# Splitting the first weight load, gating loads behind DMA transposes, and masks of a second batch on TensorE, in a fused attention and feed-forward kernel

## The chip, the cores and the metric

The kernel runs on one core of one Trainium2 chip. The metric is the time of one execution in microseconds (us) on the device; a kernel is run several times and the median is quoted with its range. Most runs of one kernel agree within about 0.5% of their median. A few runs fall into a slower state and are left out of every ratio. Runs of two kernels that were measured together are called runs of the same rounds. The span in a profile is about 2 us shorter than the time.

In this kernel TensorE does the matmuls; VectorE and ScalarE do the elementwise work and the copies; GpSimd issues most loads; SyncE issues the stores of the output and the DMA transposes. A DMA is a transfer that runs beside the engines; it "lands" when its data can be used. PSUM is the memory that matmuls write to.

## The reference, cut to what matters

Eight batches of eight heads, 576 positions, head size 64. Half of the heads use a local causal mask of 32 positions, the other half a strided one. The attention output, 4608 tokens by 512, goes through a two-layer feed-forward with a squared ReLU.

```python
scores = scale * q @ k^T                      # per batch and head
mask_local   = (rel >= 0) & (rel < 32)        # heads 0..3
mask_strided = (rel >= 0) & (pos_k % 32 == pos_q % 32)   # heads 4..7
attn = softmax(where(mask, scores, -1e9))
x = (attn @ v) as [4608, 512]
h = x @ w_in                                  # 512 x 2048
g = s * relu(h)**2 + b
out = g @ w_out                               # 2048 x 512
```

## The kernel before

The kernel computes only the blocks of scores that the masks leave. It is laid out by a small planner in Python that runs when the kernel is built. The planner keeps an estimated clock `plan.t` for TensorE, an estimated time for every result, and picks for each small task the engine that should end it first. It fixes the order of the instructions on each engine; on the chip each engine takes its instructions in that order and waits where an input is not there yet. Attention matmuls of later batches are placed between feed-forward matmuls at a pace set by `batch_ns`.

The planner's choice of an engine and place (cut):

```python
def flush(self):
    ...                                   # the task whose inputs are planned to be ready first
    eng = min(p[1], key=lambda e: max(self.free[e], r) + p[1][e])
    end = max(self.free[eng], r) + p[1][eng]
    self.free[eng] = end
    p[2](eng)                             # emits the instruction now, in that engine's order
```

The loads of a batch. GpSimd issues all of them; `landing` is the planner's guess of when they arrive. For the local heads q and k are first rearranged (`qp`, `kp`) by ScalarE or VectorE:

```python
def fetch_qk(b):
    load_qk(b)                                        # nc.gpsimd.dma_start for ql, kl, qs, ks
    for name in ("q", "k"):
        plan.done["raw", name, b] = landing(1700)
        for mm in range(2):
            pair_post(b, name, mm, ("raw", name, b))  # the copies qp <- ql and kp <- kl
    for name in ("qs", "ks"):
        arrive(both(name, b), landing(2000))
...
# fetch_qk(b + 2) is posted once attention b has all its transposes:
last_t.after = when_all("t", b, lambda b=b: plan.post(
    [("fetch_v", b + 1) if b else ("free",)] +
    [("k", (b, mk)) for mk in range(4)], {"P": 0.0},
    lambda eng: fetch_qk(b + 2), [("fetch", b + 2)]))
```

From batch 2 on, k of the strided heads is transposed by a DMA that SyncE issues; before that by TensorE:

```python
by_dma = b >= 2
def k_dma(eng):
    st["k"] = qkp.tile([128, ST, SR], FP16, tag="kTs", name="kTs")
    nc.sync.dma_start_transpose(out=st["k"], in_=ks[b % 2][:, 1024 * mm:1024 * mm + 1024])
```

Masks: in batch 0 TensorE adds a large negative number to the scores by one more matmul; later VectorE multiplies the exponentials by a mask of 0 and 1:

```python
if b == 0:
    nc.tensor.matmul(out=..., lhsT=ident[0:nk, 0:nk],
                     rhs=neg_loc if loc else neg_str, start=True, stop=False)
nc.tensor.matmul(out=..., lhsT=..., rhs=..., start=b > 0, stop=True)
```

The weights w_in come in three transfers (512, 512 and 1024 columns), and attention is paced by the work of batch 1:

```python
for c, (at, n) in enumerate(((0, 512), (512, 512), (1024, 1024))):
    nc.gpsimd.dma_start(out=w_in_sb[c], in_=wv[:, :, at:at + n])
...
batch_ns = sum(s.ns for p in att[4:8] for s in p)
```

The softmax here doesn't subtract the row's maximum and nothing guards it: scores larger than these inputs give would overflow.

Of the kernel before, what the change touches and what calls it, by code (L numbers as in the profile page):

```python
# [9 lines left out]
FP16 = mybir.dt.float16  # L10
# [100 lines left out]
def kernel(  # L111
# [11 lines left out]
    nc = tc.nc  # L123
# [4 lines left out]
    scale = 1.0 / float(np.sqrt(D))  # L128
    PS = 512
    NFT = DFF // 128  # L130
    NBLK = NTOK // PS
# [11 lines left out]
    for p in range(SQ):  # L143
        for c in range(SQ):
# [26 lines left out]

    w_in_sb = [const.tile([128, 4, n], FP16, name=f"w_in_sb{i}")
               for i, n in enumerate((512, 512, 1024))]
    w_out_sb = const.tile([128, NFT, DM], FP16)
# [91 lines left out]

    def load_w_in():
        wv = moe_w_in.rearrange("(c p) f -> p c f", p=128)
        for c, (at, n) in enumerate(((0, 512), (512, 512), (1024, 1024))):
            nc.gpsimd.dma_start(out=w_in_sb[c], in_=wv[:, :, at:at + n])  # L270

# [25 lines left out]
    def cast_v(b, loc, mm, key):  # L297
        nt, np_, dst = (LT, 128, v_loc) if loc else (ST, SQ, v_str)

        def g(eng):  # L300
# [8 lines left out]

    TB, SB, AB, F1B, F2B = 1, 2, 1, 2, 2  # L310
    ps = {tag: [psum.tile([128, PS], FP32, name=f"ps_{tag}{i}") for i in range(n)]
          for tag, n in (("t", TB), ("s", SB), ("a", AB), ("f1", F1B), ("f2", F2B))}
# [19 lines left out]
    def pair_steps(b, m):  # L332
# [54 lines left out]

        by_dma = b >= 2

        def k_dma(eng):  # L390
            st["k"] = qkp.tile([128, ST, SR], FP16, tag="kTs", name="kTs")
            nc.sync.dma_start_transpose(out=st["k"], in_=ks[b % 2][:, 1024 * mm:1024 * mm + 1024])

        if by_dma and not loc:

            plan.post([("in", "ks", b, mm), ("s", (b - 1, m), 2)], {"D": 1000.0}, k_dma,
                      [("k", id_)])
        for name in ("q", "k"):
            if by_dma and not loc and name == "k":
                continue  # L400
            gr = group_of("t", b, m, True)
            for j in range(nt):
                steps.append(trans(name, j, gr))
# [4 lines left out]
        def score(i, group):  # L408
# [3 lines left out]
            def f():  # L412
                if i % per_s == 0:
                    st["s", g] = bank(group)
                c = i % per_s * 2 * nq
                if b == 0:

                    nc.tensor.matmul(
                        out=st["s", g][0:nk, c:c + 2 * nq], lhsT=ident[0:nk, 0:nk],
                        rhs=neg_loc if loc else neg_str, start=True, stop=False)  # L420
                nc.tensor.matmul(  # L421
                    out=st["s", g][0:nk, c:c + 2 * nq], lhsT=(st["k"][:, i * nq:i * nq + nk] if loc else st["k"][:, i, 0:SQ]),
                    rhs=st["q"][:, i].rearrange("d e c -> d (e c)"), start=b > 0, stop=True)

            s = Step(f, (2 if b == 0 else 1) * (2 * nq / 2.4 + 8), needs=[("q", id_), ("k", id_)],
                     group=group if i % per_s == 0 else None)
            if i % per_s == n - 1:
# [11 lines left out]
                def ms(eng):  # L439
# [8 lines left out]
                            [("p", id_, g)])]  # L448
                if b == 0:
                    s.posts = [([key], {"A": 170 + 0.83 * 2 * n * nq}, ex, [("p", id_, g), group])]  # L450
# [95 lines left out]

        if by_dma and loc:
            plan.post([("x", id_, e, nt - 1) for e in range(2)], {"D": 1000.0}, x_dma,
                      [("xT", b, m)])
        else:  # L550
            gr = group_of("t", b, m)
            for j in range(nt):
                steps.append(xtrans(j, gr))
# [5 lines left out]
    def ff1(T, ft, ct, group, cts=(0, 1, 2, 3), early=False):  # L559
        tok0 = T * PS  # L560
        def f():
            if ft == 0 and ct == cts[0]:
                gts[T] = gp.tile([128, NFT, PS], FP16, tag="gT", name="gT")
            if ct == cts[0]:
                gts["h", T, ft] = bank(group)
            nc.tensor.matmul(  # L566
                out=gts["h", T, ft], lhsT=w_in_sb[min(ft // 4, 2)][:, ct, :].rearrange(
                    "p (c x l) -> p c l x", x=128, l=4)[:, max(ft // 4 - 2, 0), ft % 4],
# [3 lines left out]
                 for c in ((ct,) if early else range(4))]  # L572
        needs.append(("w_in", ft // 4))
        if ft == 0 and ct == cts[0] and T >= 2:
# [60 lines left out]
    def arrive(keys, at):  # L635
        for k in keys:
            plan.done[k] = at
# [12 lines left out]

    def fetch_qk(b):
        load_qk(b)
        for name in ("q", "k"):
# [45 lines left out]
    def weights_in(eng):  # L699

        nonlocal ring
        nc.gpsimd.tensor_copy(out=gate[0:64, 2:4].bitcast(FP32), in_=vl_stage[64:128, 0, 0, 0:1])
        load_w_in()
        ring = 17700.0
        for keys, cost in ([0], 2900), ([1], 2900), ([2, 3], 5000):
            arrive([("w_in", c) for c in keys], landing(cost))

    plan.done[("first",)] = 13700.0
    plan.post([("first",)], {"P": 3500.0}, weights_in, [("w",)])
    plan.done["raw", "v", True, 0] = 16200.0  # L710
# [29 lines left out]
    for b in range(B):  # L740
        for m in range(4):
            steps, last_av, last_t = pair_steps(b, m)
            att.append(steps)
            if b + 2 < B:

                last_t.after = when_all("t", b, lambda b=b: plan.post(
                    [("fetch_v", b + 1) if b else ("free",)] +
                    [("k", (b, mk)) for mk in range(4)], {"P": 0.0},
                    lambda eng: fetch_qk(b + 2), [("fetch", b + 2)]))
# [5 lines left out]
    for T in range(NBLK):  # L755
        if T == 0:

            gr = [Group(*x) for x in (("s", SB), ("s", SB), ("f1", F1B), ("f1", F1B))]
            cts = (2, 0, 1, 3)
            f1 += [ff1(T, ft, ct, gr[ft], cts, True) for ct in cts for ft in range(4)]  # L760
# [122 lines left out]
```

## Time and profile before

| | before |
|---|---|
| time, median of 3 (range) | 330.31 us (329.79 to 330.5) |
| span of the profiled run (a fourth run, 330.79 us) | 328.9 us |
| TensorE busy | 97% |
| VectorE, ScalarE, GpSimd busy | 61%, 51%, 25% |
| first feed-forward matmul | 22.19 us |

In a timeline the columns are start, duration, engine, line, operation with output and input, and in brackets the idle time before it with what ended it.

```profile
70.94 0.68 POOL L240 DMA_DIRECT2D ql<-in_q_dram  x1 [1.31 <-ACT u L584]
```

```profile
82.67 0.62 DVE L280 COPY qp<-ql 96x768 f16<-96x768 f16 x2
```

The load of q of batch 4 is issued at 70.94 us and takes 10.3 us, so it lands at 81.26. VectorE copies it at 82.67 without a wait. Between the landing and the copy there are 1.4 us of slack.

### The profile page before, as it was taken

What the parts mean: (1) busy time and instruction counts of PE and PEld (TensorE: products, weight loads), DVE (VectorE), ACT (ScalarE), POOL (GpSimd) and SP (SyncE); (2) the same over time, 40 slices, a digit from 0 to 9 for tenths busy, and PEclk for the clock granted to TensorE, in tenths of its full rate; (3) what the DMA queues carried; (4) which work ended last, traced back from release to release, by engine and by line L of the source; (5) the groups of instructions that cost most, each with busy time, mean ns of one, the idle gap of its engine ahead of it and who ended that gap; (6) DMA issues with size and microseconds to landing.
All of it is one profiled execution on the core that took longest, in us unless ns stands there. A gap on an engine that the chain in (4) does not pass through costs nothing.

```text
span 328.9 us, 6347 instructions
## 1 busy us (share of the span) xinstructions
PE 319.1 (97%) x2407; PEld 182.0 (55%) x2407; DVE 201.4 (61%) x553; ACT 168.8 (51%) x319; POOL 82.2 (25%) x112
## 2 busy tenths in 40 slices
PE   8969999999999999999999999999999999999994
PEld 3755655666556666556656556655444544444442
DVE  5665866689877867876777878786332432333211
ACT  2755954499727987754664445553532433233100
POOL 7361549746126434412710000000000000000000
PEclk9998999999999999999999999999999999999999
DMA  8999999999999999949994320111001000100021
GB/s 119 172 177 205 214 154 171 210 170 158 137 146 147 135 58 182 134 64 101 148 117 55 81 84 2 51 52 64 2 32 64 32 34 33 64 31 35 32 98 64
DMA packets 74472, 33.13 MB, mean 101 GB/s; under 512 B 55882, under 2 KB 68810, under 8 KB 74442
## 3 DMA queue, kind: packets, MB, share of 16 engines
q0 software_dynamic: 49984, 18.65, 55.0%
q1 hardware_dynamic: 24458, 14.07, 21.1%
q8 instruction: 19, 0.31, 0.4%
q14 instruction: 11, 0.09, 0.1%
HBM read 38.15 MB, written 9.44 MB: 145 GB/s over the span
## 4 chain that ended last, share of the span: by engine, by line
PE 89%; DMA 6%; DVE 2%; ACT 1%; issue 1%; SPq 0%; POOL 0%; POOLq 0%; DVEq 0%
PE ps_f L601 38%; PE ps_f L566 36%; PE ps_s L421 4%; PE ps_a L473 4%; PE ps_t L350 3%; DMA w_in_sb<-in_moe_w_in_dram 3%; DMA w_out_sb<-in_v_dram 2%; PE ps_t L521 2%; DMA ql<-in_q_dram 1%; PE ps_a L624 1%; PE ps_s L566 1%; ACT u L584 1%; ACT qD_loc L280 1%; DVE qD_str L280 1%; PE ps_f L473 0%
## 5 line engine op out<-in xcount | busy, mean ns | idle before, releaser
L566 PE MATMUL ps_f<-xT,w_in_sb 128*128 128x512 f16 x568 | 154.0, 381 | 0.0
L601 PE MATMUL ps_f<-w_out_sb,gT 128*128 128x512 f16 x576 | 151.8, 379 | 0.4 <-DVE gT L590 0.4
L584 ACT ACTIVATE u<-ps_f 128x512 f16<-128x512 f32 x138 | 82.0, 597 | 83.3 <-PE ps_f L566 61.1
L590 DVE TENSOR_TENSOR gT<-u 128x512 f16<-128x512 f16 x144 | 59.4, 420 | 55.3 <-ACT u L584 54.6
L566 PEld LDWEIGHTS <-w_in_sb 128*128 128x128 f16 x576 | 61.7, 114 | 43.9 <-DMA w_in_sb<-in_moe_w_in_dram 2.1
L601 PEld LDWEIGHTS <-gT 128*128 128x128 f16 x576 | 54.2, 98 | 50.4 <-DVE gT L590 1.1
L435 ACT ACTIVATE pt<-ps_s 128x384 f16<-128x384 f32 (+2 forms) x96 | 44.8, 488 | 15.7 <-PE ps_s L421 15.1
L473 PEld LDWEIGHTS <-pt 72*72 72x72 f16 (+1 forms) x448 | 35.2, 119 | 13.2 <-DVE x_nat L499 0.2
L612 DVE SCALAR_TENSOR_TENSOR o<-ps_f,s_sb,bcs 128x512 f32<-128x512 f32 x36 | 26.8, 745 | 20.6 <-PE ps_f L601 20.3
L499 DVE TENSOR_TENSOR x_nat<-ps_a,rec 72x256 f16<-72x256 f32 (+1 forms) x76 | 35.0, 461 | 1.7
L488 DVE RECIPROCAL rec<-ps_a 72x4 f32<-72x4 f32 (+1 forms) x76 | 13.7, 181 | 18.5 <-PE ps_a L473 16.3
L258 POOL DMA_DIRECT2D v_loc<-in_v_dram x28 | 24.3, 875 | 1.7 <-issue 0.9
L263 POOL DMA_DIRECT2D v_str<-in_v_dram x16 | 13.5, 844 | 44.5 <-PE ps_a L473 22.8
L473 PE MATMUL ps_a<-v_str,pt 72*72 72x65 f16 x204 | 20.9, 196 | 0.0
L421 PE MATMUL ps_s<-qD_str,kTs 128*72 128x144 f16 x128 | 20.1, 226 | 0.2 <-ACT kTs L280 0.2
L280 ACT COPY xT<-ps_t 128x576 f16<-128x576 f16 x16 | 10.2, 637 | 14.1 <-PE ps_t L521 14.0
L421 PEld LDWEIGHTS <-kTs 128*72 128x72 f16 x128 | 13.0, 113 | 5.7 <-ACT kTs L280 0.4
L473 PE MATMUL ps_a<-v_loc,pt 128*96 128x65 f16 x150 | 16.2, 203 | 0.0
L421 PE MATMUL ps_s<-qD_loc,kT_loc 128*128 128x192 f16 x96 | 16.0, 246 | 0.0
L443 DVE TENSOR_TENSOR pt<-pt,mask_str 72x432 f16<-72x432 f16 (+1 forms) x42 | 14.3, 349 | 2.8 <-ACT pt L435 2.5
L443 DVE TENSOR_TENSOR pt<-pt,mask_loc 128x384 f16<-128x384 f16 x42 | 14.2, 351 | 2.2 <-ACT pt L435 1.8
L521 PEld LDWEIGHTS <-x_nat 72*128 72x128 f16 (+1 forms) x152 | 9.9, 102 | 6.5 <-DVE x_nat L499 1.1
(87 smaller groups left out, 253.6 us busy)
## 6 DMA issues: line engine op xcount, KB each, us to landing
out_dram<-o SPq DMA_DIRECT2D x36, 256.0 KB, 2.0
ql<-in_q_dram POOLq DMA_DIRECT2D x8, 288.0 KB, 6.6
kl<-in_k_dram POOLq DMA_DIRECT2D x8, 288.0 KB, 7.5
v_loc<-in_v_dram POOLq DMA_DIRECT2D x28, 80.0 KB, 11.4
w_out_sb<-in_moe_w_out_dram POOLq DMA_DIRECT2D x4, 512.0 KB, 12.0
qs<-in_q_dram POOLq DMA_DIRECT2D x6, 288.0 KB, 8.6
ks<-in_k_dram POOLq DMA_DIRECT2D x6, 288.0 KB, 9.5
v_str<-in_v_dram POOLq DMA_DIRECT2D x16, 72.0 KB, 4.6
```

The lines of the kernel that those rows point to most:

```text
L258: nc.gpsimd.dma_start(out=vl[:, h, 1:LT, 0:D], in_=rest[:, h])
L280: {"A": nc.scalar.copy, "V": nc.vector.tensor_copy, "P": nc.gpsimd.tensor_copy}[eng](**kw)
L421: nc.tensor.matmul(out=st["s", g][0:nk, c:c + 2 * nq], lhsT=(st["k"][:, i * nq:i * nq + nk] if loc else st["k"][:, i, 0:SQ]), rhs=st["q"][ ...
L435: nc.scalar.activation(out=pt[0:nk, 0:2 * n].rearrange("k t c -> k (t c)"), in_=st["s", g][0:nk, 0:2 * n * nq], func=AF.Exp, scale=scale)
L443: nc.vector.tensor_tensor(out=pt[0:nk, 0:2 * n], in0=pt[0:nk, 0:2 * n], in1=mask, op=ALU.mult)
L473: nc.tensor.matmul(out=st["a"][0:nq, j % per, :], lhsT=st["pt", g][0:nk, i, :], rhs=vt[0:nk, 2 * mm + e, j, :])
L499: nc.vector.tensor_tensor(out=st["x"][:, j0:j0 + per, 64 * e:64 * e + 64], in0=st["pa", e, j][0:nq, 0:per, 0:D], in1=st["rec", e, j][0:nq, ...
L566: nc.tensor.matmul(out=gts["h", T, ft], lhsT=w_in_sb[min(ft // 4, 2)][:, ct, :].rearrange("p (c x l) -> p c l x", x=128, l=4)[:, max(ft // ...
L584: nc.scalar.activation(out=gts["u", T, ft], in_=gts["h", T, ft], func=AF.Relu)
L590: nc.vector.tensor_tensor(out=gts[T][:, ft, :], in0=u, in1=u, op=ALU.mult)
L601: nc.tensor.matmul(out=gts["o", T, ts], lhsT=gts[T][:, ft, ts * 128:(ts + 1) * 128], rhs=w_out_sb[:, ft, :], start=(ft == 0), stop=(ft == ...
L612: nc.vector.scalar_tensor_tensor(out=o, in0=gts["o", T, ts], scalar=s_sb[:, 0:1], in1=bcs, op0=ALU.mult, op1=ALU.add)
```

## The change

The intent: let TensorE start on the feed-forward when the first 128 KB of w_in are there; take mask work off a nearly full VectorE in batch 1; and let a DMA transpose of k land before the loads of the next batch fill the DMA engines. The k transposes of batch 2 also go back to TensorE. The diff, cut to its core:

```diff
+    FIRST = (2, 0, 1, 3)
...
-    def load_w_in():
+    def load_w_in(first):
         wv = moe_w_in.rearrange("(c p) f -> p c f", p=128)
-        for c, (at, n) in enumerate(((0, 512), (512, 512), (1024, 1024))):
-            nc.gpsimd.dma_start(out=w_in_sb[c], in_=wv[:, :, at:at + n])
+        if first:
+            for c in FIRST:
+                nc.gpsimd.dma_start(out=w_in0[c], in_=wv[:, c, 0:512])
+        else:
+            nc.gpsimd.dma_start(out=w_in_sb[0], in_=wv[:, :, 512:1024])
+            nc.gpsimd.dma_start(out=w_in_sb[1], in_=wv[:, :, 1024:2048])
...
+    PE_MASK = 2
...
-        by_dma = b >= 2
+        k_by_dma, x_by_dma = b >= 3, b >= 2
 
         def k_dma(eng):
             ...
+            loaded[b, "kTs", mm] = st["k"]
...
-                if b == 0:
+                if b < PE_MASK:                      # the mask matmul; and where VectorE's mask falls away
...
     def fetch_qk(b):
+        for mm in range(2):
+            if (b - 1, "kTs", mm) in loaded:
+                nc.gpsimd.tensor_copy(out=gate[0:1, 2 + mm:3 + mm],
+                                      in_=loaded[b - 1, "kTs", mm][0:1, 0, 0:1])
         load_qk(b)
...
-                    [("k", (b, mk)) for mk in range(4)], {"P": 0.0},
+                    [("k", (bk, mk)) for bk in (b, b + 1 if b > 1 else b) for mk in range(2, 4)],
+                    {"P": 0.0},
```

Below, "the gate" is the eight one-element copies on GpSimd together with the later trigger (last hunk). Each copy reads a transposed k and so makes GpSimd wait until that transpose has landed. "The split" is the four transfers of w_in. "The pace" is `batch_ns`: since the mask matmuls of batch 1 now count in it, it grows by 2144 ns, although nobody edited it.

More of the change, by code (lines that the diff above doesn't have):

```diff
@@ L170 @@
     b_sb = const.tile([128, 1], FP32)
-    w_in_sb = [const.tile([128, 4, n], FP16, name=f"w_in_sb{i}")
-               for i, n in enumerate((512, 512, 1024))]
+    w_in0 = [const.tile([128, 512], FP16, name=f"w_in0{i}") for i in range(4)]
+    w_in_sb = [const.tile([128, 4, n], FP16, name=f"w_in_sb{i}") for i, n in ((1, 512), (2, 1024))]
     w_out_sb = const.tile([128, NFT, DM], FP16)
@@ L392, in k_dma @@
             nc.sync.dma_start_transpose(out=st["k"], in_=ks[b % 2][:, 1024 * mm:1024 * mm + 1024])
-        if by_dma and not loc:
+            loaded[b, "kTs", mm] = st["k"]
+        if k_by_dma and not loc:
             plan.post([("in", "ks", b, mm), ("s", (b - 1, m), 2)], {"D": 1000.0}, k_dma,
@@ L398, in pair_steps @@
         for name in ("q", "k"):
-            if by_dma and not loc and name == "k":
+            if k_by_dma and not loc and name == "k":
                 continue
@@ L422, in f @@
                     out=st["s", g][0:nk, c:c + 2 * nq], lhsT=(st["k"][:, i * nq:i * nq + nk] if loc else st["k"][:, i, 0:SQ]),
-                    rhs=st["q"][:, i].rearrange("d e c -> d (e c)"), start=b > 0, stop=True)
-            s = Step(f, (2 if b == 0 else 1) * (2 * nq / 2.4 + 8), needs=[("q", id_), ("k", id_)],
+                    rhs=st["q"][:, i].rearrange("d e c -> d (e c)"), start=b >= PE_MASK, stop=True)
+            s = Step(f, (2 if b < PE_MASK else 1) * (2 * nq / 2.4 + 8), needs=[("q", id_), ("k", id_)],
                      group=group if i % per_s == 0 else None)
@@ L448, in score @@
                             [("p", id_, g)])]
-                if b == 0:
+                if b < PE_MASK:
                     s.posts = [([key], {"A": 170 + 0.83 * 2 * n * nq}, ex, [("p", id_, g), group])]
@@ L545, in x_dma @@
                 in_=st["x"].rearrange("p t d -> p (t d)"))
-        if by_dma and loc:
+        if x_by_dma and loc:
             plan.post([("x", id_, e, nt - 1) for e in range(2)], {"D": 1000.0}, x_dma,
@@ L566, in f @@
             nc.tensor.matmul(
-                out=gts["h", T, ft], lhsT=w_in_sb[min(ft // 4, 2)][:, ct, :].rearrange(
+                out=gts["h", T, ft], lhsT=(w_in_sb[min(ft // 4, 2) - 1][:, ct, :] if ft > 3 else w_in0[ct]).rearrange(
                     "p (c x l) -> p c l x", x=128, l=4)[:, max(ft // 4 - 2, 0), ft % 4],
@@ L572, in ff1 @@
                  for c in ((ct,) if early else range(4))]
-        needs.append(("w_in", ft // 4))
+        needs.append(("w_in", ft // 4) if ft > 3 else ("w_in0", ct))
         if ft == 0 and ct == cts[0] and T >= 2:
@@ L702, in weights_in, with more_weights @@
         nc.gpsimd.tensor_copy(out=gate[0:64, 2:4].bitcast(FP32), in_=vl_stage[64:128, 0, 0, 0:1])
-        load_w_in()
-        ring = 17700.0
-        for keys, cost in ([0], 2900), ([1], 2900), ([2, 3], 5000):
+        load_w_in(True)
+        ring = 18000.0
+        for c in FIRST:
+            arrive([("w_in0", c)], landing(650))
+    def more_weights(eng):
+        load_w_in(False)
+        for keys, cost in ([1], 3000), ([2, 3], 5100):
             arrive([("w_in", c) for c in keys], landing(cost))
     plan.done[("first",)] = 13700.0
-    plan.post([("first",)], {"P": 3500.0}, weights_in, [("w",)])
+    plan.post([("first",)], {"P": 2800.0}, weights_in, [("w1",)])
+    plan.post([("w1",)] + both("vl", 0), {"P": 1500.0}, more_weights, [("w",)])
     plan.done["raw", "v", True, 0] = 16200.0
@@ L758 @@
             gr = [Group(*x) for x in (("s", SB), ("s", SB), ("f1", F1B), ("f1", F1B))]
-            cts = (2, 0, 1, 3)
+            cts = FIRST
             f1 += [ff1(T, ft, ct, gr[ft], cts, True) for ct in cts for ft in range(4)]
```

## The prediction

> **What bounds the kernel now.** I read the page's engine table first, then the slices, then the chain of waits from the start to 45 us, then the stretches below, and last the timelines of TensorE and of the GpSimd queue for the same time.
>
> ```profile
> PE 319.1 (97%) x2407; PEld 182.0 (55%) x2407; DVE 201.4 (61%) x553; ACT 168.8 (51%) x319; POOL 82.2 (25%) x112
> ...
> PEclk9998999999999999999999999999999999999999
> ```
>
> TensorE is busy for 97% of the span. Matmul ends are modelled, so I tested this with start-to-start times: a 512-column matmul follows another after 0.216 us almost everywhere. Of the feed-forward layers alone there are 576 + 576 such matmuls, 249 us. Only more matmul work or a TensorE gap can move the end; a saving on another engine counts only if it closes a gap. The one dip of the granted clock is in the fourth slice, and the chain of waits says why:
>
> ```profile
> 6.80 6.26 DMA w_out_sb<-in_v_dram
> 13.06 0.02 issue
> 13.08 0.02 POOLq L702
> 13.10 0.08 issue
> 13.18 0.18 POOL gate L702
> 13.37 0.28 issue
> 13.64 8.50 DMA w_in_sb<-in_moe_w_in_dram
> 22.14 0.05 issue
> 22.19 0.62 PE ps_s L566 x2
> ```
>
> Columns are start, duration, what. The first quarter of w_in is one transfer, issued at 13.64 and landed at 22.14; the first feed-forward matmul waits for all of it. The next view (busy us of each engine per stretch, granted clock, DMA share, GB/s) puts sizes to it:
>
> ```profile
> 20.20:22.20 2.00, 0.05 (x2) 0.01 (x1) 0.91 (x3) 0.40 (x2) 0.72 (x2) 1.00 1.09 159
> 22.20:28.40 6.20, 5.63 (x37) 3.08 (x38) 1.59 (x5) 1.73 (x6) 1.12 (x2) 0.72 1.15 208
> 28.40:43.30 14.90, 14.37 (x124) 8.84 (x123) 13.32 (x34) 12.58 (x24) 6.34 (x9) 1.00 1.15 211
> 43.30:66.00 22.70, 22.32 (x194) 12.75 (x192) 13.09 (x43) 10.03 (x18) 17.32 (x21) 1.00 1.43 175
> 66.00:100.00 34.00, 33.59 (x299) 20.45 (x299) 28.64 (x87) 24.11 (x49) 13.98 (x18) 1.00 1.48 148
> 100.00:230.00 130.00, 130.00 (x1116) 78.58 (x1114) 99.09 (x279) 79.68 (x150) 29.77 (x38) 1.00 0.86 93
> ```
>
> TensorE stands still for 2 us, then works at a clock of 0.72 for 6 us. From 28.4 to 43.3 VectorE and ScalarE are nearly full (13.3 and 12.6 of 14.9) while TensorE hardly waits. After 43 us nothing but TensorE is full, though the DMA engines stay loaded until about 100 us.
>
> ```profile
> 22.19 0.62 PE L566 MATMUL ps_s<-xT,w_in_sb 128*128 128x512 f16 x2 [1.95 <-DMA w_in_sb<-in_moe_w_in_dram]
> ...
> 23.87 0.66 PE L521 MATMUL ps_t<-ident,x_nat 96*128 96x96 f16 x6 [0.57 <-DVE x_nat L499]
> ...
> 28.24 5.34 PE L566 MATMUL ps_f<-xT,w_in_sb 128*128 128x512 f16 x24
> ```
>
> The second gap, 0.57 us, is a consequence of the first: attention matmuls that were ready stand behind the waiting one in TensorE's order.
>
> **What the Trainium skill says.** "TensorE: Matmul & The Clock Gate", section "What's actually happening": the clock falls to half after an idle window of about 3.4 us, and the windows run freely. The trace agrees in kind: five 512-column matmuls between 24.3 and 27 us took 0.41 to 0.43 us of TensorE's time instead of 0.216, though the idle time was only 1.95 + 0.57 us. The same page, "Back-to-back issue gap", gives N/2.4 + 2.5 ns: 82.5 ns for 192 columns and 62.5 for 144. The trace has 82 and 63 to 65. "DMA: Bandwidth & Descriptors", "Issuing engines are not separate DMA queues": all queues share the same 16 engines. The trace agrees: the twelve k transposes, all of one size, took from 2.6 to 12.4 us from issue to landing, the long ones behind GpSimd's loads. The same page, "Anatomy of one DMA", gives 2.0 us plus bytes over 436 GB/s; here 512 KB cost about 3.2 us at the margin (second quarter of w_in landed at 14.41 + 11.0 = 25.4, the first at 22.14), so I use 3.2.
>
> **Part 1, w_in in four transfers.** Each quarter of the quarter is 128 KB and costs 3.2/4 = 0.8 us at the margin. Counted back from 22.14 they should land near 19.7, 20.5, 21.3 and 22.1 (estimate). TensorE has attention work until 20.24, so the first feed-forward matmul can start about 2 us earlier, and ready attention work no longer stands behind it. The gross prize in the 20 to 27 us stretch is 1.95 + 0.57 us idle and 6 x 0.2 = 1.2 us lost to the half clock: 3.7 us.
>
> Not all of it stays. The other three quarters of w_in still follow in the same stream, and their issue moves from 14.4 to about 18.6 (four issues of 0.76 us and four casts of v of 0.5 us now come first). The third transfer lands now at 15.16 + 15.1 = 30.3; I see nothing that brings it forward. Its first user is matmul 17 of the row of 24 at 28.24, so at 28.24 + 16 x 0.216 = 31.7. There are only 1.4 us of slack there. A TensorE that is 3.7 us earlier runs into this landing and keeps 1.4 us. So is q of batch 1, whose copy began at 32.0. Part 1 is worth **-1.4 us**, perhaps -2.
>
> **Part 2, masks of batch 1 by TensorE.** Added: two local pairs x 6 = 12 mask matmuls of 192 columns at 0.082 = 0.98 us, and 2 x 8 = 16 of 144 columns at 0.065 = 1.04 us. All on the bounding engine: **+2.0 us**. Removed: 2 x 3 + 2 x 3 = 12 mask multiplications on VectorE at 0.35 = 4.2 us, and one hop (about 0.4 us) in each chain from exponential to the product with v. VectorE was nearly full until 43 us, so this helps the gaps there: 0.38 us at 36.99 and 0.48 us at 39.78 (spacing beyond the matmul's own time). It is worth perhaps **-0.5 us**.
>
> **Part 3, k transposes.** Batch 2 goes back to TensorE: 2 x 8 = 16 transposes at 0.032 = **+0.5 us**, and two copies of 0.45 to 0.64 us on ScalarE or VectorE. Two DMA transposes fall away at 62 to 74 us, where they took 10 us each. From batch 3 on, GpSimd waits for the landed transposes before it issues the loads of the next batch, by eight tiny copies. The transposes then take nearer 2.6 us and the loads come later. TensorE shows no wait for a DMA-transposed k now, so I book 0 for both.
>
> **Part 4, what moves unasked.** The kernel's own planner spaces attention by the work of batch 1, which now counts its mask matmuls. The built order of the changed kernel shows attention in blocks of four to eight matmuls where it stood singly between feed-forward ones, and ending somewhat earlier. Spacing costs TensorE nothing (an attention matmul took the same time before another as before a feed-forward one), but evacuation gets burstier. Between 43 and 100 us the spacing shows 2.8 us of small gaps; 0.56 at 66.0 waits for ScalarE's copy of x, 0.53 at 90.2 for VectorE's square. Batch 1 leaves sooner and batch 2 is attended earlier, so I book **-1.3 us** here, the least certain term.
>
> **Sum.** -1.4 + 2.0 - 0.5 + 0.5 - 1.3 = -0.7 us. Against 330.3 that is about 329.5.
>
> **Rivals.** (a) The early start survives whole, because the third w_in transfer lands earlier too or the planner finds other work: -3.7 instead of -1.4, so about 327. For it: the DMA rate dips around 20 us, and the transfer is no larger. Against it: the stream is already at 1.15 and 208 GB/s behind that point. (b) The wait only moves: TensorE now idles before the second or third transfer with no filler matmuls (the planner inserts those only among the first 16 feed-forward steps), and the clock halves once more, costing up to 1.7 us in a 3.4 us window. Then +2.5 of added work stands against nothing: about 332. (c) The new gate on GpSimd delays loads so that q, k or v arrive late after 90 us; each batch has some 27 us for loads that take 10 to 15, so I expect no wait. If it bites, each of four batches could lose a microsecond: 333 or more. (d) Bursts of attention fill ScalarE and gaps appear between 100 and 200 us, where there are only about 1.6 us now: +1 to +3.
>
> **Range and chances.** The terms are each a few tenths to 2 us and partly cancel. Two per cent is 6.6 us; all gaps after 22 us together are about 7.5 us, so a 2% gain would need nearly all of them closed and no price for 2.5 us of added matmuls: 2%. A 2% loss needs rivals (b), (c) and (d) together: 2%. Eight times in ten I expect 327.2 to 331.8.
>
> **What would show it.** Part 1: the first feed-forward matmul near 20 us, no 0.72 clock stretch, and a TensorE wait for the third w_in transfer or for q of batch 1 near 29 to 32 us. If that wait is missing and everything at 44 us is over 1.5 us earlier, the retained gain was mis-sized. Part 2: 28 more mask matmuls of 0.08 and 0.065 us in the 30 to 46 us stretch, and VectorE visibly below 13.3 of 14.9. Part 3: landing times of k transposes near 3 us, and 16 more matmuls into ps_t. Part 4: fewer and shorter gaps from 43 to 100 us; new ones after 100 us would make me wrong upward.

## The result, and the profile after

The changed kernel takes 334.52 us (334.1 to 335.44, six runs) against 330.05 us (328.55 to 330.5, six runs) for the kernel before in the same rounds. The ratio is 1.0148, with a 95% interval of 1.0122 to 1.0174. Ratios here are the mean time of one kernel's fast runs over that of the other's of the same rounds, so not quite the ratio of the medians. Within 2%, as predicted, but slower by 1.5% and outside my range, which ended at 331.8 us.

The engine table of the changed kernel, its chain of waits by engine and line, and one group of instructions (busy time and mean ns; then idle time of the engine before them and what ended it):

```profile
PE 321.3 (97%) x2452; PEld 183.7 (55%) x2452; DVE 196.1 (59%) x542; ACT 168.5 (51%) x320; POOL 85.6 (26%) x123
...
PE 73%; DMA 15%; issue 4%; DVE 4%; POOL 2%; ACT 1%; SPq 0%; POOLq 0%; DVEq 0%
PE ps_f L609 34%; PE ps_f L574 28%; DMA ql<-in_q_dram 9%; PE ps_a L481 3%; PE ps_s L429 3%; PE ps_t L357 2%; DMA vs<-in_v_dram 2%; DMA w_out_sb<-in_v_dram 2%; DMA kTs<-ks 2%; PE ps_t L529 1%; PE ps_a L632 1%; DVE qp L286 1%; PE ps_s L426 1%
...
L663 POOL COPY gate<-kTs 1x1 f16<-1x1 f16 x8 | 2.7, 333 | 39.0 <-DMA kTs<-ks 38.8
```

The first line says almost nothing: TensorE is still 97% busy. The chain says where to look. In the first trace of the kernel before, 6% of the chain was DMA; now it is 15%, and 9% of the span is the load of q, which was 1%. That is a place to look and no proof: in the second trace of the unchanged kernel (e5) DMA is 10% and the load of q 8%. The last line names the new instruction on GpSimd: eight copies of one element, 2.7 us of work, 38.8 us of waiting.

The stretches of the prediction, now of the changed kernel (from:to, length, then busy us of PE, PEld, DVE, ACT, POOL with counts, clock, DMA share, GB/s):

```profile
20.20:22.20 2.00, 1.30 (x20) 0.76 (x17) 1.56 (x7) 1.28 (x6) 2.00 (x5) 1.00 1.22 200
22.20:28.40 6.20, 6.20 (x38) 3.43 (x37) 3.23 (x8) 3.53 (x9) 1.08 (x2) 1.00 1.15 209
28.40:43.30 14.90, 14.14 (x147) 9.76 (x146) 10.27 (x23) 11.84 (x23) 6.92 (x10) 1.00 1.14 210
...
66.00:100.00 34.00, 31.59 (x307) 19.92 (x306) 26.67 (x84) 24.68 (x49) 11.89 (x17) 1.00 1.47 131
100.00:230.00 130.00, 128.56 (x1095) 76.96 (x1094) 96.06 (x278) 76.52 (x146) 33.00 (x45) 1.00 0.90 90
```

Up to 66 us these figures are what the change was made for: TensorE works from about 20 us on and at full clock, and VectorE falls from 13.3 to 10.3 us of the 14.9. (The unchanged kernel in e5 starts almost as early, and has 11.7 us for VectorE.) Then TensorE stands still for 2.4 us of the 34 where it had lost 0.4 (1.1 in e5), and for 1.4 us after 100 us where it had lost none in either trace. The loss is not where the work was added.

The chain of waits of the changed kernel at the first of these places (start, duration, what):

```profile
73.59 3.40 DMA kTs<-ks
...
77.04 0.18 POOL gate L663
77.22 4.81 issue
...
82.58 4.59 DMA ql<-in_q_dram
...
87.20 1.04 DVE qp L286 x2
88.24 0.33 DVE gT L598
88.57 0.35 DVE x_nat L507
...
88.96 0.30 PE ps_a L481 x4
```

And two engines in the same time, first GpSimd, then VectorE:

```profile
77.04 0.18 POOL L663 COPY gate<-kTs 1x1 f16<-1x1 f16 x1 [9.58 <-DMA kTs<-ks]
82.06 0.18 POOL L663 COPY gate<-kTs 1x1 f16<-1x1 f16 x1 [4.83 <-DMA kTs<-ks]
82.58 0.69 POOL L242 DMA_DIRECT2D ql<-in_q_dram  x1 [0.35 <-issue]
```

```profile
87.20 1.04 DVE L286 COPY qp<-ql 96x768 f16<-96x768 f16 x2 [1.68 <-DMA ql<-in_q_dram]
```

Read in order of time: GpSimd stands from 67.5 us before its first gate copy (9.58 us of waiting), which the first k transpose ends at 77.04, and again until 82.06 for the second. The transposes themselves take 3.4 and about 3.2 us; they are issued at 73.59 and 78.84, where SyncE comes to them (in e9, with no copies that wait, at 73.23 and 78.48). So some 8 of these 14.6 us are a wait for transposes that were not issued yet. Only then may GpSimd issue the load of q of batch 4, at 82.58 instead of 70.94. It lands at 87.18. VectorE's order was fixed at build time, and in it the copy of q stands where the planner thought q would be there. VectorE reaches it at about 85.5 and waits 1.68 us with other work ready behind it. One piece of that work is the normalisation `x_nat`, which frees the only PSUM bank of the attention outputs (a bank is one block of PSUM), and TensorE's next attention matmul needs that bank: it waits 1.88 us and starts at 88.96.

That an engine cannot pass over a waiting instruction is what the Trainium skill says ("Perfetto Trace Analysis", section "Tensor Engine Instruction (MATMUL, LD_WEIGHTS)": ScalarE, VectorE and GpSimd are strictly first in, first out). The trace agrees: the square and the normalisation behind `qp` come only after it in the chain, at 88.24 and 88.57.

To put sizes on this I summed, over each trace, the time from the start of one matmul to the start of the next, less the first one's own pace (columns/2.4 + 2.5 ns; 34 or 42 ns for the 65-column ones, whose medians are 34 and 45). What is left are TensorE's gaps; a gap is put where the next matmul starts. "Gaps, all" is what the other rows leave of the span, the first 14 us included (the last matmul, 0.2 us, stands in two rows of every column). "Warming matmuls" are those on a tile of ones, with no use for the result. This is my own calculation from the traces' start times, of one profiled run each; "before again" is experiment e5, a second trace of the unchanged kernel, and "without copies" is experiment e9.

| us | before | before again | changed | changed without copies |
|---|---|---|---|---|
| matmul work | 305.31 | 305.31 | 307.82 | 307.82 |
| warming matmuls | 5.63 | 5.63 | 5.80 | 5.80 |
| gaps, all | 13.42 | 12.09 | 14.44 | 10.16 |
| of them 14 to 30 us | 5.70 | 2.63 | 2.59 | 2.14 |
| 30 to 80 us | 1.98 | 3.02 | 1.92 | 1.90 |
| 80 to 100 us | 0.88 | 1.97 | 3.05 | 1.01 |
| 120 to 140 us | 0.03 | 0.04 | 0.86 | 0.07 |
| 160 to 180 us | 0.05 | 0.03 | 1.14 | 0.07 |
| after the last start | 4.56 | 4.56 | 4.50 | 4.21 |
| span | 328.9 | 327.6 | 332.6 | 328.0 |

Against "before again", the changed kernel's span is longer by 2.5 us of work, 0.2 us of warming matmuls and 2.35 us of gaps, 5.0 us in all with the tail.

### The profile page after: what moved, and what is told of

It reads as the page before. It is cut to its first block, busy times and chain, and to the rows that moved or that the text cites. A ratio compares the mean times of both kernels' runs of the same rounds, so it can differ in the third digit from the quotient of the medians.

```text
span 332.6 us, 6436 instructions
## 1 busy us (share of the span) xinstructions
PE 321.3 (97%) x2452; PEld 183.7 (55%) x2452; DVE 196.1 (59%) x542; ACT 168.5 (51%) x320; POOL 85.6 (26%) x123
## 4 chain that ended last, share of the span: by engine, by line
PE 73%; DMA 15%; issue 4%; DVE 4%; POOL 2%; ACT 1%; SPq 0%; POOLq 0%; DVEq 0%
PE ps_f L609 34%; PE ps_f L574 28%; DMA ql<-in_q_dram 9%; PE ps_a L481 3%; PE ps_s L429 3%; PE ps_t L357 2%; DMA vs<-in_v_dram 2%; DMA w_out_sb<-in_v_dram 2%; DMA kTs<-ks 2%; PE ps_t L529 1%; PE ps_a L632 1%; DVE qp L286 1%; PE ps_s L426 1%; DVE o L620 1%; DVE pt L451 1%
## 5 line engine op out<-in xcount | busy, mean ns | idle before, releaser
L609 PE MATMUL ps_f<-w_out_sb,gT 128*128 128x512 f16 x576 | 147.6, 379 | 0.2 <-DVE o L620 0.2
L574 PE MATMUL ps_f<-xT,w_in_sb 128*128 128x512 f16 x432 | 115.1, 379 | 0.4 <-DMA w_in_sb<-in_moe_w_in_dram 0.3
L574 PEld LDWEIGHTS <-w_in_sb 128*128 128x128 f16 x432 | 46.3, 113 | 34.5 <-DMA w_in_sb<-in_moe_w_in_dram 0.7
L481 PEld LDWEIGHTS <-pt 72*72 72x72 f16 (+1 forms) x448 | 29.0, 120 | 13.8 <-issue 3.6
L574 PE MATMUL ps_f<-xT,w_in 128*128 128x512 f16 x136 | 35.4, 379 | 0.1
L574 PEld LDWEIGHTS <-w_in 128*128 128x128 f16 x144 | 15.4, 114 | 10.3
L481 PE MATMUL ps_a<-v_str,pt 72*72 72x65 f16 x204 | 15.3, 197 | 2.8 <-DVE x_nat L507 2.8
L429 PE MATMUL ps_s<-qD_str,kTs 128*72 128x144 f16 x128 | 15.5, 226 | 0.2 <-ACT kTs L286 0.2
L429 PE MATMUL ps_s<-qD_loc,kT_loc 128*128 128x192 f16 x96 | 14.9, 246 | 0.7 <-ACT pt L443 0.5
L429 PEld LDWEIGHTS <-kTs 128*72 128x72 f16 x128 | 11.7, 114 | 5.0 <-ACT kTs L286 0.4
L663 POOL COPY gate<-kTs 1x1 f16<-1x1 f16 x8 | 2.7, 333 | 39.0 <-DMA kTs<-ks 38.8
L286 ACT COPY qD_loc<-ps_t 64x576 f16<-64x576 f16 x18 | 11.4, 632 | 2.1 <-PE ps_t L357 2.0
## 6 DMA issues: line engine op xcount, KB each, us to landing
w_out_sb<-in_moe_w_out_dram POOLq DMA_DIRECT2D x4, 512.0 KB, 11.6
```

The lines of the kernel that those rows point to most:

```text
L286: {"A": nc.scalar.copy, "V": nc.vector.tensor_copy, "P": nc.gpsimd.tensor_copy}[eng](**kw)
L429: nc.tensor.matmul(out=st["s", g][0:nk, c:c + 2 * nq], lhsT=(st["k"][:, i * nq:i * nq + nk] if loc else st["k"][:, i, 0:SQ]), rhs=st["q"][ ...
L481: nc.tensor.matmul(out=st["a"][0:nq, j % per, :], lhsT=st["pt", g][0:nk, i, :], rhs=vt[0:nk, 2 * mm + e, j, :])
L574: nc.tensor.matmul(out=gts["h", T, ft], lhsT=(w_in_sb[min(ft // 4, 2) - 1][:, ct, :] if ft > 3 else w_in0[ct]).rearrange("p (c x l) -> p c ...
L609: nc.tensor.matmul(out=gts["o", T, ts], lhsT=gts[T][:, ft, ts * 128:(ts + 1) * 128], rhs=w_out_sb[:, ft, :], start=(ft == 0), stop=(ft == ...
```

## The experiments

The expectations name theories by number or letter. Theory 1: the gate is the loss, by late loads. Theory N: the late w_in in the first trace of the kernel before was an unlucky run. Theory Q: the loss goes through VectorE's fixed order, at the copy of q. Theory C: of the gate's two parts, the copies cost it all. All runs gave a correct result, and all profiled runs were in the fast state, but for e5, a single run to which no state can be given.

### e1: the change without its gate

```diff
     def fetch_qk(b):
-        for mm in range(2):
-            if (b - 1, "kTs", mm) in loaded:
-                nc.gpsimd.tensor_copy(out=gate[0:1, 2 + mm:3 + mm], in_=...)
         load_qk(b)
...
-                    [("k", (bk, mk)) for bk in (b, b + 1 if b > 1 else b) for mk in range(2, 4)],
+                    [("k", (b, mk)) for mk in range(4)],
```

> The changed kernel with GpSimd's wait for landed k transposes taken out, and the loads of q and k triggered by the same condition as in the kernel before; everything else stays. Theory 1 (the late loads cost it): the gaps of TensorE after 80 us, 4.1 us more than before, go, and the time falls from 334.5 to about 330.4, within 0.3% of the kernel before. Theory 2 (the planner's new pacing asks for attention too soon, and the loads are only where that shows): the gaps stay to more than half, 332.5 or more. Added matmul work (2.5 us) stays in both.

330.96 us (330.0 to 332.8) against 330.04 in the same rounds; ratio 1.0026 (0.9992 to 1.0061). The loss of 1.5% shrinks to nothing that can be told from zero. Theory 1 stands.

### e2: the change at the pace of the kernel before

```diff
-    batch_ns = sum(s.ns for p in att[4:8] for s in p)
+    batch_ns = sum(s.ns for p in att[4:8] for s in p) - 2144.0
```

> The changed kernel with the planner's measure of a batch put back to what it was without the mask matmuls (2144 ns less), the gate kept. Theory 1 (the gate makes loads late whatever the pace): about 334, at most 1 us better than the changed kernel, with GpSimd still waiting over 30 us for k transposes. Theory 2 (pacing): about 330.5, and TensorE's gaps after 80 us gone.

338.93 us (336.71 to 341.23), ratio 1.0268 (1.0225 to 1.0312). That is worse than the change itself; the pacing theory, which wanted it better, falls, and Theory 1's "about 334" is missed too. GpSimd now waits 59.1 us at its eight gates instead of 38.8, and the gaps from 120 to 160 us are 7.2 us. I had no theory that foretold this. It fits the gate: attention placed later makes the transposes later and the gate longer. That was not tested by itself.

### e3: the kernel before with the split alone

The edit is the w_in part of the change, on the kernel before.

```diff
-        for c, (at, n) in enumerate(((0, 512), (512, 512), (1024, 1024))):
-            nc.gpsimd.dma_start(out=w_in_sb[c], in_=wv[:, :, at:at + n])
+        if first:
+            for c in FIRST:
+                nc.gpsimd.dma_start(out=w_in0[c], in_=wv[:, c, 0:512])
+        else:
+            ...
```

> The kernel before with only the first quarter of w_in in four transfers. Theory A (the early start is kept whole, as the trace of the changed kernel suggests with 3.2 us less of gaps before 80 us): about 326.9, ratio 0.990. Theory B (my prediction: it runs into the third w_in transfer and keeps 1.4 us): about 328.7, ratio 0.996.

330.73 us with a wide scatter (329.3 to 333.87), ratio 1.0032 (0.9985 to 1.0078). No gain: neither theory's ratio, 0.990 or my 0.996, lies in the interval. The profiled run was the slowest of the six, and its VectorE timeline shows the same sore place with no gate at all:

```profile
84.94 0.63 DVE L286 COPY qp<-ql 96x768 f16<-96x768 f16 x2 [1.95 <-DMA ql<-in_q_dram]
```

VectorE comes to this copy no earlier than in the first trace (82.99 against 82.67). It is the load of q that is later: issued at 72.46 instead of 70.94, it takes 12.5 us instead of 10.3. So the 1.4 us of slack can go without a gate; why the load was later here I have not tested.

### e4: the kernel before with the gate alone

```diff
     def fetch_qk(b):
+        for mm in range(2):
+            if (b - 1, "kTs", mm) in loaded:
+                nc.gpsimd.tensor_copy(out=gate[0:1, 2 + mm:3 + mm], in_=...)
         load_qk(b)
...
-                    [("k", (b, mk)) for mk in range(4)],
+                    [("k", (bk, mk)) for bk in (b, b + 1 if b > 0 else b) for mk in range(2, 4)],
```

> The kernel before with only the gate: GpSimd waits for the landed k transposes of a batch, and the loads are triggered one batch's transposes later. Masks and w_in as before. Theory 1 (the gate alone costs it): 333 to 335, GpSimd waits over 30 us for k transposes, TensorE's gaps after 70 us grow by 3 to 5 us. Theory 2 (only with the new pacing): within 1 us of the kernel before, 329 to 331.

338.07 us (335.31 to 339.87), ratio 1.0233 (1.0192 to 1.0274), with no work added to TensorE (305.31 us as before) but 18.9 us of gaps. The waits of GpSimd (us in total, times, longest us):

```profile
POOL gate L656 <- DMA kTs<-ks: 47.5, 10, 8.1
```

Ten waits (here batch 2 has DMA transposes too), 47.5 us, the longest 8.1. The gate is enough for a loss by itself. With e1 it is settled both ways round that the gate makes the loss; which of its two parts does is left to e9.

### e5: the kernel before, once more

The kernel is unchanged.

> The kernel before once more, unchanged, for a second trace. Theory N (the 4.4 us of gaps at 22 to 30 us in the first trace of it were an unlucky landing of w_in, not its rule): first quarter of w_in lands near 20 us as it did in the run with only the gate, gaps of 1 to 2 us in that stretch, no stretch at half clock, and yet a time near 330. Theory R (they are the rule): landed near 22 us, gaps over 3.5 us.

329.37 us, one run, inside the range of the kernel before (328.49 to 331.51 in these rounds). This is the run that takes away much of the ground of my Part 1. The first feed-forward matmul, and the stretch from 20.2 to 28.4 us, in this trace:

```profile
19.78 0.62 PE L566 MATMUL ps_s<-xT,w_in_sb 128*128 128x512 f16 x2
```

```profile
20.20:28.40 8.20, 7.79 (x53) 4.13 (x51) 5.51 (x16) 4.24 (x11) 1.78 (x4) 1.00 1.10 193
```

The same instructions as in the trace that I predicted from, but the first quarter of w_in lands 6.1 us after its issue instead of 8.5, the matmul starts at 19.78 instead of 22.19, and the clock stays at 1.00 in this stretch. In e4 and e6, whose start is the same, it takes 5.6 and 5.5 us. The late landing is not a single accident, though. In e11 below every engine has the same order of instructions as in the kernel before up to 69 us, and it takes 7.3 us; the first feed-forward matmul, and the stretch from 22.2 to 28.4 us, there:

```profile
21.46 0.62 PE L566 MATMUL ps_s<-xT,w_in_sb 128*128 128x512 f16 x2 [1.14 <-DMA w_in_sb<-in_moe_w_in_dram]
```

```profile
22.20:28.40 6.20, 5.63 (x35) 2.68 (x33) 2.05 (x6) 2.23 (x7) 0.61 (x2) 0.72 1.15 210
```

So two of the five traces with this start have the late landing and the clock of 0.72, and three have neither. These two runs have a mean clock of 0.992; of the 43 fast runs of the kernel before in the experiments' rounds four have 0.992 or less, a hint that it is the rarer case. Theory N, with this limit.

Nor did its late start cost the first trace much in the end: it has 3.4 us more gaps than e5 before 30 us, and 2.1 us fewer from 30 to 100 us (2.9 against 5.0), where work that is further ahead runs into other waits. The chain of e5 passes there through two loads of q, 12.51 us from 17.75 and 10.25 us from 70.75, and VectorE waits at the very copy that had 1.4 us of slack in the first trace:

```profile
81.02 0.63 DVE L280 COPY qp<-ql 96x768 f16<-96x768 f16 x2 [0.49 <-DMA ql<-in_q_dram]
```

### e6: the kernel before with masks of batch 1 by TensorE

```diff
-                if b == 0:
+                if b < PE_MASK:          # PE_MASK = 2, at each of the four places
```

> The kernel before with only the masks of batch 1 moved to TensorE (which also raises the planner's measure of a batch). Theory P (TensorE is the bound, so its added work comes out in full): 332, ratio 1.006. Theory V (VectorE's 4.2 us less and the new pacing pay for it): 330 or less, ratio 1.000 or below, with fewer gaps from 30 to 100 us.

332.06 us (331.33 to 332.88, and one slow run), ratio 1.0049 (1.0019 to 1.0079), so +1.6 us (0.6 to 2.6); work on TensorE is 1.99 us more. The price of the mask matmuls may be paid in full or in part. The edit also raises the pace, as in the change, so what is measured is both together.

### e7: the change with its gate, but the planner told that q and k come later

If VectorE's fixed order carries the loss, a planner that expects q later puts the copy later, and the same gate should hurt less.

```diff
     def fetch_qk(b):
+        LATE = 2500.0 if b >= 4 else 0.0
...
-            plan.done["raw", name, b] = landing(1700)
+            plan.done["raw", name, b] = landing(1700) + LATE
...
-            arrive(both(name, b), landing(2000))
+            arrive(both(name, b), landing(2000) + LATE)
```

> The changed kernel, gate kept, with only the planner told that q and k of batches 4 to 7 come 2.5 us later than it assumed; loads and their trigger stay. Theory Q (what costs is that the copy of q stands in VectorE's order ahead of work that is ready, and waits there for the load): the waits of VectorE and ScalarE for q and k fall from about 10 us to under 3, TensorE's gaps after 80 us from 5.1 to under 2, time 331 to 332. Theory L (the loads are simply too late for TensorE, whatever stands where): the gaps move to other places and the time stays within 1 us of 334.5.

332.43 us (331.13 to 333.14), ratio 1.0065 (1.0035 to 1.0095) where the change has 1.0148. The wait of VectorE in question (us in total, times, longest us):

```profile
DVE qp L286 <- DMA ql<-in_q_dram: 2.6, 2, 1.6
```

GpSimd waits nearly as long as before (34.4 us against 38.8), but VectorE waits 2.6 us for q where it waited 6.8 us, and more than half of the loss is gone. So a late load by itself need not cost much; the cost seems to arise where the copy stands too early in VectorE's order. That fits Theory Q for the larger part: the 2.6 us are no more than VectorE waits for q in the unchanged kernel in e5 (3.1 us), and TensorE's gaps after 80 us fall from 5.4 to 2.2 us. The time and the gaps stay a little above what I had expected (331 to 332, under 2 us), and a ratio of 1.0065 still lies above 1. The planner also lays out everything after these loads anew, so e7 does not show the place of the copy alone.

### e8: the kernel before with the split and the raised pace

```diff
 (the split as in e3, and)
-    batch_ns = sum(s.ns for p in att[4:8] for s in p)
+    batch_ns = sum(s.ns for p in att[4:8] for s in p) + 2144.0
```

> Only w_in in four transfers, with the planner's measure of a batch raised as the masks raise it, but no mask matmuls added, no gate, k of batch 2 by DMA. Theory W (the pacing that came with the masks is what kept the early start of w_in in the run without the gate): about 327.5 to 328.5, gaps at 80 to 90 us below 1 us instead of 4.6, better than both kernels. Theory S (only the relief of VectorE from the masks kept it): 330 to 331 as with the split alone.

330.95 us (329.07 to 331.94, and two slow runs); ratio 0.9992 (0.9952 to 1.0031). Neither a gain nor a loss: Theory W's 327.5 to 328.5 is missed. As a search for a better kernel it failed.

### e9: the change without the eight copies, the later trigger kept

```diff
     def fetch_qk(b):
-        for mm in range(2):
-            if (b - 1, "kTs", mm) in loaded:
-                nc.gpsimd.tensor_copy(out=gate[0:1, 2 + mm:3 + mm], in_=...)
         load_qk(b)
```

> The changed kernel without GpSimd's eight copies that wait for landed k transposes, but with the later trigger of the loads kept (q and k of a batch are issued once the k transposes of the batch before are issued). Theory C (the wait for landing costs): q and k are issued earlier by the 3 to 5 us of a transposition, time near 331.5. Theory T (the order costs: the loads stand behind transposes that themselves wait for the scores of an earlier batch to free the buffer of k): q of batch 4 still issued after 78 us against 71 before, and the time stays within 1 us of 334.5.

This is the cleanest of the twelve. The planner books nothing for the copies, so the built order of TensorE, VectorE, ScalarE and SyncE is the same as in the changed kernel, instruction by instruction, and GpSimd's differs by the eight copies only. It takes 330.21 us (329.78 to 331.11) against 330.88; ratio 0.999 (0.9963 to 1.0017). That is better than Theory C's 331.5, and Theory T, the later trigger as the cost, falls. TensorE at the critical place, in the changed kernel and then here:

```profile
85.40 1.68 PE L574 MATMUL ps_f<-xT,w_in_sb 128*128 128x512 f16 x7
88.96 0.30 PE L481 MATMUL ps_a<-v_str,pt 72*72 72x65 f16 x4 [1.88 <-DVE x_nat L507]
```

```profile
85.04 1.68 PE L574 MATMUL ps_f<-xT,w_in_sb 128*128 128x512 f16 x7
86.55 0.30 PE L481 MATMUL ps_a<-v_str,pt 72*72 72x65 f16 x4
```

The same two rows, 3.56 us from start to start with the copies and 1.51 without. GpSimd issues the load of q of batch 4 at 68.15 us, 14.4 us earlier than with the copies (I had expected 3 to 5), and VectorE copies it at 85.08 with no wait:

```profile
68.15 0.68 POOL L242 DMA_DIRECT2D ql<-in_q_dram  x1 [0.55 <-DVE qp L286]
```

The landing times of the k transposes (us, minimum, median, maximum) turn this round. First the changed kernel, then e9:

```profile
DMA to landing us min/median/max: 2.6/2.7/4.4
```

```profile
DMA to landing us min/median/max: 2.9/7.6/9.2
```

So the gate does what it was for, and the transposes are nearly three times as fast with it. But nobody was waiting for them: in e9 no engine's wait ends at the landing of a k transpose. Theory C: by the ratios the copies cost 1.0148 - 0.999 = 1.6%, about 5.2 us (4.0 to 6.4, an estimate from the two intervals); by the medians 334.52 - 330.21 = 4.3 us.

### e10 and e11: raised pace and a late plan, with and without the split

```diff
-    batch_ns = sum(s.ns for p in att[4:8] for s in p)
+    batch_ns = sum(s.ns for p in att[4:8] for s in p) + 2144.0
 (and LATE as in e7, from batch 3 on; e10 has the split of e3 as well, e11 not)
```

> An attempt at a version that beats both: w_in in four transfers, the raised pace without mask matmuls, no gate, k by DMA from batch 2, and the planner told that q and k of batches 3 to 7 come 2.5 us later. If the copies placed too early are the cause of the 3 us spread between runs, time 327.5 to 328.5 with a small spread, ratio about 0.993. If not, 330 to 331 as with the raised pace alone.

> The same without the split of w_in: the kernel before with the raised pace and the later assumed landing of q and k. If the split is worth something once the later stalls are gone, this is 0.5 to 2 us slower than the run with the split; if w_in lands near 20 us in most runs and its split is hidden, the two are equal within 0.5 us.

330.07 us (329.08 to 331.53), ratio 0.9984 (0.9955 to 1.0013), with the split; 330.04 us (329.25 to 331.22), ratio 0.998 (0.9954 to 1.0006), without. The two differ by the split alone and are equal within their scatter. It is worth nothing that these runs can show, here as in e3. The 327.5 to 328.5 with a small spread that I had hoped for in e10 did not come, so copies placed too early are not shown to be the cause of the spread. The profiled run of e11, with the late landing that e5's section shows, is the slowest of its six, 331.22; the other five end by 330.36. In such a run the split may save about a microsecond; that was not tested.

### e12: the change without the copies, and with the masks of batch 1 back on VectorE

```diff
 (the gate's copies removed as in e9, and)
-    PE_MASK = 2
+    PE_MASK = 1
...
-    batch_ns = sum(s.ns for p in att[4:8] for s in p)
+    batch_ns = sum(s.ns for p in att[4:8] for s in p) + 2144.0
```

> The changed kernel without the eight waiting copies and with the masks of batch 1 back on VectorE, the planner's raised pace kept: w_in in four transfers, k by TensorE for batches 0 to 2, later trigger. TensorE has 2.0 us less to do than in the run with the copies alone taken out. If VectorE's 12 more mask multiplications are hidden, 328.2 and a ratio of 0.993; if they open gaps between 40 and 90 us, 330 or more and the masks by TensorE were paid for.

330.95 us (330.07 to 334.13), ratio 1.0015 (0.9957 to 1.0073), against 0.999 for e9. TensorE has 2.0 us less work and 2.6 us more gaps, 1.5 of them from 44 to 100 us. So taking the masks back gains nothing that can be seen here, although in e6, from the kernel before, adding them cost 1.6 us. The intervals of e9 and e12 overlap; I don't claim which is better. No version that I ran is clearly faster than the kernel before. The best ratios are those of e9, e10 and e11, within 0.2% of it; all three beat the changed kernel.

## Why the prediction was wrong, step by step

**Where it failed: the gate in Part 3.** I wrote "TensorE shows no wait for a DMA-transposed k now, so I book 0 for both". The first half is right and shows that the gate could gain nothing. The second does not follow: what a gate costs depends on who waits for what is held back behind it. In place of the 0 the runs showed 4.3 to 5.2 us (e9), and e4 shows a loss from the gate alone. That one term is about the whole error: 334.5 less 329.5 is 5.0.

**Rival (c) was the answer, and I dismissed it with the wrong number.** I set 27 us per batch against 10 to 15 us of loads. The number to look for was the slack between a landing and its first reader in that reader's fixed order: 81.26 and 82.67 in the trace that I had, 1.4 us (and none in e5), against a delay of 11.6 us in the issue. That the load is then quicker (4.6 us instead of 10.3) returns only half of it. "If it bites, each of four batches could lose a microsecond" was then about right in size: of the 4.3 us of gaps by which the changed kernel exceeds e9, 2.0 lie from 80 to 100 us, 0.8 near 138 and 1.1 near 167: three of the four batches.

**Part 1, -1.4 us: measured as none.** Alone it gave a ratio of 1.0032 with an interval that leaves 0.9958 out (e3), and e10 equals e11. The step that failed is the "gross prize" of 3.7 us: it was read from one trace in which the first quarter of w_in was late, as in two of five traces (e5). Against the repeated trace, the changed kernel's first feed-forward matmul is earlier by 0.6 us (19.18 against 19.78), not 3. Two landings were misjudged as well: the four parts came at 17.7 to 19.7 us (issue plus 4.2 to 4.6), not at 19.7 to 22.1, and the third transfer at 29.2, not 30.3. The limit that I foresaw is there. TensorE's rows with waits at about 30 us, in the changed kernel:

```profile
29.20 1.70 PE L574 MATMUL ps_f<-xT,w_in_sb 128*128 128x512 f16 x7 [0.25 <-DMA w_in_sb<-in_moe_w_in_dram]
...
31.22 0.43 PE L357 MATMUL ps_t<-ident,qp 96*128 96x96 f16 x6 [0.32 <-DVE qp L286]
```

It runs into a later w_in transfer and into q of batch 1, as written.

**Part 2, +2.0 us: right; -0.5 us: not shown.** The work is 1.99 us more. e6 measured +1.6 us (0.6 to 2.6), with the raised pace in it. My terms for the masks and the pace together, Parts 2 and 4, are +2.0 - 0.5 - 1.3 = +0.2 us, below that interval; so in e6 at least one of the two reliefs did not come, and it does not tell which. Parts do not simply add, either: in the setting of e12 the same masks cost nothing that can be seen. The planner lays out everything anew for each edit, which may be why; that was not tested.

**Part 3, +0.5 us for the transposes of batch 2: right in count.** The total of matmul work rose by 2.51 us, 2.0 of masks and 0.5 of transposes. The landing times near 3 us came as foretold (median 2.7 us, from 7.5).

**Part 4, -1.3 us: not settled.** With the copies out, gaps from 44 to 100 us are 1.7 us in e9 and 3.0 us in e5, a difference of 1.3; in the first trace they are 2.0. (The prediction's 2.8 us is a reading on another base: with the formula's 29.6 ns for a 65-column matmul I get 2.9; the table's paces, 34 and 42 ns, are nearer to what these matmuls took.) These are single traces, and the same kernel differs by 1.0 between two of them. In the changed kernel as it stands they are 3.7 us, so the gain, if it is one, was spent at the gate.

**The other rivals.** (a) did not come: no run was near 327. (b) did not come: the clock is 1.00 in every stretch shown of the changed kernel. (d) did not come: the gaps after 100 us go with the copies (e9), so they are no bursts of attention.

**Open.** Why the old pace with the gate is so much worse (e2). Whether the later trigger alone does anything: e1 and e9 differ by it, 1.0026 and 0.999, with overlapping intervals. Why w_in was late in the first trace and in e11. Whether the raised pace is worth anything: in e6 it did not pay, e8 and e11 show no gain. And the sum without the gate's loss, 329.5 us, agrees with e9's 330.21 us partly by luck: one of its terms, Part 1, was wrong.

## What to carry to other kernels

A wait put on an engine that issues loads costs nothing by itself, but it delays every load behind it; so before adding one, read the slack between each later load's landing and its first reader, in that reader's fixed order, and not only the waits that exist now. A transfer that got three times as fast is no gain if nobody waited for it. And take a second trace before you size a prize from one wait for a transfer, or a slack from one landing: here the same instructions gave a landing of 8.5 us and one of 6.1 us, and a slack of 1.4 us and none, in runs whose times lie within 0.5% of each other.

## What the Trainium skill lacked or had wrong

- "DMA: Bandwidth & Descriptors", section "Anatomy of one DMA": from its formula a 512 KB transfer takes 3.2 us (an estimate: 2.0 us plus 512 KB over 436 GB/s). From issue to landing it took 8.5, 6.1, 5.6, 5.5 and 7.3 us in five traces with the same instructions up to there (before, e5, e4, e6, e11). The page gives no spread for its formula and no figure for one load among other loads in flight.
- The same page, section "Issuing engines are not separate DMA queues", says that queues share the engines. I found no page with what this does to a waiting time: the k transposes, all of one size, took a median of 2.7 us with GpSimd's loads held back and 7.6 us without (e9), up to 12.4 us in the kernel before.
- "TensorE: Matmul & The Clock Gate", section "What's actually happening": it gives an idle window of about 3.4 us. In the first trace the granted clock fell to 0.72 over 6.2 us after idle times of 1.95 and 0.57 us, and in e11 to the same 0.72 after 1.14 and 0.57 us, so no wait of 3.4 us was needed; in the changed kernel a wait of 1.88 us left it at 1.00.
- That a wait on GpSimd put there to order one transfer also holds back all loads that it issues later follows from the strict order cited above, but no page that I found says it of loads, or what it can cost: here 38.8 us at eight copies of one element, and 1.6% of the time.
